# Three buffers instead of two for the weight-conversion tile, four instead of five for the activation's first temporary

## Chip, cores and metric

One core of one Trainium2 chip runs the whole program. The metric is the device time of one execution in microseconds, as a median over runs. The engines are TensorE (PE, with its weight loads as PEld), VectorE (DVE), ScalarE (ACT), GpSimd (POOL) and SyncE (SP), which issues every DMA here.

## What is computed

A causal attention with a multiplicative decay is followed by two dense feed-forward layers. The weights of the layers come as 64-bit floats, which the kernel itself turns into 32-bit floats.

```python
scores = q @ k.T / sqrt(D) + (cum[i] - cum[j])      # cum = cumsum(log f), causal
x = softmax(scores) @ v                             # 4 batches, 8 heads, 576 x 64
h = x @ w_in1                                       # 2304 x 512 @ 512 x 2048
x = where(h >= 1, h, where(h <= -1, 0, (h+1)**2/4)) @ w_out1
h = x @ w_in2
out = (P(h) / (Q(h) + 1e-6)) @ w_out2               # P cubic, Q quadratic in |h|
```

## The kernel before

Every product that must be exact to about 32 bits is made of three matmuls: each operand is split into a high part (a cast to fp32r on ACT) and a low part (a subtraction on DVE or POOL), and wl·xh, wh·xl and wh·xh are accumulated in PSUM.

**Attention** works on 16 pairs of heads, 9 blocks of rows each. **The first layer** is tiled into 16 groups g of 128 hidden columns and five chunks x of tokens (four of 512, one of 256). For one chunk and one group, `gemm_in` (L735) makes the hidden tile h in PSUM with 12 matmuls, an activation follows, `split_g_hi` (L745) and `split_g_lo` (L749) split the result, and `gemm_out` (L829, in the second layer L831) adds 12 matmuls to the output accumulators. Groups 0 to 3 of chunks 0 and 1 are done during the attention; their `gemm_out` is L816. After the attention come groups 0 to 3 of chunks 2 and 3, then groups 4 to 15 of chunks 0 to 3, then the short chunk, then the second layer, chunk after chunk. One chunk's input is split by L720 (ACT, xh) and L724 (DVE, xl), one step for each of four slices kk. The split tiles have one buffer each, so the next chunk's steps wait until the last group's `gemm_in` of the chunk before has read the slice.

**Weights.** A unit is one half (0: w_in, 1: w_out) of one group's weights. `w_raw` (L83) loads the 512 KB of its 64-bit words into a tile "raw", of which there are two. `w_steps` makes 32-bit floats of it: s0 (L93, ACT) takes a tile "d" and writes the absolute value's upper word, s1 to s4 (L97, L101, L107, L113, all DVE) work on it in place, and s4 frees raw. Then one of two things happens. Either the unit is split at once: L127 (ACT) writes wh and L131 (POOL) writes wl from it, and L131 frees d. Or the unit is stored to DRAM by L140, and d is free when the store has landed; `w_load` (L145) brings it back later, half 0 into a "d" tile and half 1 into a "raw" tile, and L127 and L131 split it. Units of groups 0 to 3 of layer 1 (8 units) are converted and split in the attention, groups 4 to 8 (10 units) are converted and stored there. After the attention groups 9 to 15 (14 units) are converted and split, and the 32 units of layer 2 are converted and stored; these are loaded again while the short chunk runs.

**Activation temporaries.** In the first layer `a11` (L754, DVE) takes a tile t0 for the clamped h, `a12` (L759, ACT) squares it into t1, which is the last use of t0, and `a21` (L763, DVE) is the last reader of h. In the second layer `b_abs` (L770, ACT) takes t0, t1 and t2; the last reader of t0 is `b_ln`/`b_exp` (L791, L794, ACT), and h is last read by `b_t4` (L805, DVE). h has four buffers (HB = 4) after the attention.

**Order.** Nothing is reordered by hand. Each piece of work is a task with an engine, an assumed duration, a key (its turn), tasks it depends on, and tags of buffers that it takes and frees. `plan` goes through simulated time and takes, again and again, the task with the smallest start time plus a small weight times its key; a task that takes a tag can't start before a buffer of it is free. The counts of buffers in `N_BUF` and in `bufs.update` are thus the planner's picture of the pools. The engines' programs are emitted in the planned order, once for the attention with what is mixed into it, and once for all that follows. On the chip every engine runs its program in order, and waits by semaphores where a tile is still in use.

```python
free_at = max(free_at, sorted(bufs[tag])[k - 1])
...
at = max(clock[eng], free_at)
...
cand = (choice[1] + turn + wk * key, key, n, choice[1], choice[2])
```

The keys of the units: a unit of the attention is loaded with its key less 6 and stored with its key plus 3; a unit of layer 2 has key base + 20 + i, is loaded with that less 4 and stored with that plus 1. Successive units of the attention that are stored are 6.4 apart in key.

Of the kernel before, what the change touches and what calls it, by code (L numbers as in the profile page):

```python
# [7 lines left out]
F32 = mybir.dt.float32  # L8
# [10 lines left out]
def kernel(ctx, tc, qT, kT, v, f, w_in1, w_out1, w_in2, w_out2, a, b, out):  # L19
    nc = tc.nc  # L20
    PE, ACT, DVE, POOL, SP = nc.tensor, nc.scalar, nc.vector, nc.gpsimd, nc.sync
    B, H, S = f.shape
    D = v.shape[2] // 2
    NT, DM = out.shape
# [4 lines left out]
    P = 128  # L29
# [11 lines left out]
    W_EARLY = 4  # L41
# [2 lines left out]
    CM, CE = 80, 144  # L44
    PB = 6
    FILL = 2
    SB, TB_, OB, RB = 4, 2, 2, 2
    KM, KEX, KT, KC, KV, KR, KX, PKL, LK, FE, FS = 0.0, 1.0, 4.0, 4.0, 7.0, 2.0, 9.0, 7.0, 14.0, 170.0, 40.0
    I_K, I_Q = 4.4, 5.2
# [27 lines left out]
    wpool = {}  # L77
# [8 lines left out]
    def w_steps(m, g, half):  # L86

        at = {}

        def s0():  # L90
            at["t"] = wst.pop((m, g, half))
            at["d"] = wpool["stage"].tile([P, DM], F32, tag="d", name="wd", bufs=2)
            ACT.activation(at["d"][:], at["t"][:, :, 1].bitcast(F32), AF.Abs)  # L93

        def s1():
            d = at["d"][:]
            DVE.tensor_scalar(out=d, in0=d, scalar1=W_MIN, scalar2=W_MAX, op0=ALU.max, op1=ALU.min)  # L97

        def s2():
            di = at["d"][:].bitcast(I32)  # L100
            DVE.tensor_scalar(  # L101
                out=di, in0=di, scalar1=3, scalar2=0x3FFFFFF8, op0=ALU.logical_shift_left, op1=ALU.bitwise_and
            )

        def s3():
            di = at["d"][:].bitcast(I32)
            DVE.scalar_tensor_tensor(  # L107
                out=di, in0=at["t"][:, :, 1], scalar=-1073741824, in1=di, op0=ALU.bitwise_and, op1=ALU.bitwise_or
            )

        def s4():
            di = at["d"][:].bitcast(I32)
            DVE.scalar_tensor_tensor(  # L113
                out=di, in0=at["t"][:, :, 0], scalar=29, in1=di, op0=ALU.logical_shift_right, op1=ALU.bitwise_or
            )
            wst[m, g, half] = at["d"][:]

        return [s0, s1, s2, s3, s4]

    def w_split(m, g, half):  # L120
# [20 lines left out]

    def w_load(m, g, half):
        tag, shape = (("d", [P, DM]), ("raw", [P, 2 * DM]))[half]
        t = wpool["stage"].tile(shape, F32, tag=tag, name=f"wf{m}_{g}_{half}", bufs=2)[:, 0:DM]
        SP.dma_start(t, wfd[m, g, half])  # L145
        wst[m, g, half] = t

# [2 lines left out]
    stage = wpool["stage"] = ctx.enter_context(tc.tile_pool(name="stage", bufs=1))  # L150
# [19 lines left out]
    for j in range(2):  # L170
        t = tri2[j * QB:(j + 1) * QB, 192:256]
# [13 lines left out]
    cb = [ap1.tile([P, 3, S], F32, name=f"cb{n}") for n in range(2)]  # L185
# [9 lines left out]
    half = ap1.tile([P, 2], F32, name="half")  # L195
# [51 lines left out]
    SF = 4  # L247
    XR = 4
    XA = 3
    KMK = 2.0  # L250
    LX = 4.0
    T0 = 1.5
    N_BUF = dict(S=SB, T=TB_, O=OB, P=PB, PT0=1, PT1=1, q=2, k=2, qs=2, ks=2, v=2, R=RB, x=1, cb=2, g=W_EARLY, c=2, s=SF, xa=XA, xr=XR, po=2, raw=2, d=2)
    LAT = {"pe": 0.2, "act": 0.2, "dve": 0.2, "pool": 0.2, "sp": 0.0, "init": 0.0}

    def task(key, eng, dur, fn, deps=(), take=(), free=()):
# [6 lines left out]
    shape = {}  # L263
# [7 lines left out]
    bufs = {}  # L271
# [94 lines left out]
    xa = {}  # L366
# [310 lines left out]
    t = task(-99, "init", 1.0, lambda: None)  # L677
    t = task(-99, "pe", 0.4 * WARM, lambda: warm(WARM), (t,), ("T",), ("T",))
    task(-99, "pe", 0.22 * WARM2, lambda: warm(WARM2), (t,), ("T",), ("T",))
    x = ft[:, 0, :].bitcast(F32)  # L680
    t = task(-99, "init", 2.86, lambda: None)
    t = task(-99, "dve", 0.37, lambda x=x: f_clip(x), (t,))
    t = task(-99, "act", 0.57, lambda x=x: ACT.activation(x, x, AF.Ln), (t,))
    t = task(-99, "dve", 1.35, lambda x=x: f_scan(cum, x), (t,))
    t = task(-99, "act", 0.57, c_hi, (t,))
    t2 = task(-98, "act", 0.57, c_all, (t,))
    t = tid[0, "c"] = task(-99, "dve", 0.67, c_lo, (t,))
# [3 lines left out]
    t = task(20, "sp", [(0.55, 0.01)] * 2, ab_load)  # L691
    t = task(24, "act", 0.4, ab_fn, (t,))
    for e, fn in root_steps():
        t = task(30, e, 0.3 if e == "act" else 0.17, fn, (t,))
# [31 lines left out]
    hps, gt, mid, acc, po = {}, {}, {}, {}, {}  # L726
# [24 lines left out]
    def a11(g, n):  # L751
        c = t_new(g, "t0", n, 2 if filling else TN[0])
        s = t_new(g, "t1", n, SF if filling else TN[1])
        DVE.tensor_scalar(out=c, in0=hps[g], scalar1=-1.0, scalar2=1.0, op0=ALU.max, op1=ALU.min)  # L754
        mid[g] = [s, c]
# [117 lines left out]
    wd, stored = {}, {}  # L873
# [15 lines left out]
    for n, u in enumerate(units):  # L889
# [3 lines left out]
        t = convert(u, key, step, 6)  # L893
# [8 lines left out]
    pieces = []  # L902
    for x in range(FILL):
        pieces += [(CH[x] / 4, "x", x, kk) for kk in range(KD)]
# [5 lines left out]
    for size, kind, x, k in pieces:  # L910
# [3 lines left out]
        if kind == "x":  # L914
            t = xload = task(key - LX, "sp", ld(n), lambda x=x, k=k: x_load(x, k), xstores(x, k) + [xload], ("xr",))
            t = task(key, "act", cost("act", n), lambda x=x, k=k: split_x_hi(x, k), [t] + ([fid[kind, x, 0]] if k else []), ("x",) if k == 0 else ())
            fid[kind, x, k] = task(key, "dve", cost("dve", n), lambda x=x, k=k: split_x_lo(x, k), (t,), (), ("xr",))
        elif kind == "g":
            deps = [fid["x", x, kk] for kk in range(KD)] + [wd[0, k, 0], fid.get((kind, x - 1, k)), fid.get(("in", x, k - 1))]
            t = None  # L920
            for kk in range(KD):
                t = task(key, "pe", mm(n, 3), lambda x=x, k=k, kk=kk: gemm_in(0, x, k, (kk,)), deps if t is None else (t,),
                         ("O",) if t is None else (), ("x",) if k == W_EARLY - 1 and kk == KD - 1 else ())
            fid["in", x, k] = t
            t = task(key, "dve", cost("dve", n), lambda k=k, n=n: a11(k, n), (t,), ("c", "s"))
            t = task(key, "act", cost("act", n), lambda k=k: a12(k), (t,), (), ("c",))
            t = task(key, "dve", cost("dve", n), lambda k=k: a21(k), (t,), (), ("O",))
            t = task(key, "act", cost("act", n), lambda k=k, n=n: split_g_hi(k, n), (t,), ("g",))
            fid[kind, x, k] = task(key, "pool", cost("pool", n), lambda k=k: split_g_lo(k, POOL), (t,), (), ("s",))
        else:  # L930
            deps = [fid["g", x, g] for g in early] + [wd[0, g, 1] for g in early] + [fid.get((kind, x, k - 1))]
            t = None
            for part in range(3):
                t = task(key, "pe", mm(n, W_EARLY), lambda x=x, k=k, part=part: gemm_out1(x, early, k, part),
                         deps if t is None else (t,), ("O",) if t is None else (), ("g",) * W_EARLY if k == KD - 1 and part == 2 else ())
            fid[kind, x, k] = t
            t = task(key, "act", cost("act", n, "ps"), lambda x=x, k=k: part_out(x, k), (t,), ("po",), ("O",))
# [3 lines left out]
    for kk in range(KD):  # L941
        n = CH[FILL]
        t = xload = task(FE + PX, "sp", ld(n), lambda kk=kk: x_load(FILL, kk), xstores(FILL, kk) + [xload], ("xr",))
        t = task(FE + PX, "act", cost("act", n), lambda kk=kk: split_x_hi(FILL, kk), [t] + sx0[:1], ("x",) if kk == 0 else ())
        sx0.append(task(FE + PX, "dve", cost("dve", n), lambda kk=kk: split_x_lo(FILL, kk), (t,), (), ("xr",)))
    TN = 5, 5, 5
    GB = 3
    HB = 4
    KO = 4, 8
# [11 lines left out]

    bufs.update({tag: [T0] * n for tag, n in N_BUF.items()})
    order_ = plan(0, WK)
# [10 lines left out]

    passes = [(0, x, early) for x in range(FILL, HEAD)] + [(0, x, late) for x in range(HEAD)]
    passes += [(0, x, range(NF)) for x in range(HEAD, NCH)]
# [12 lines left out]
    base = NS  # L989
    t_end = max(done[tid[NPAIR - 1, f"O{g}"]] for g in range(2)) + 0.2  # L990
    bufs.clear()
    bufs.update({tag: [t_end] * k for tag, k in dict(h=HB, g=GB, t0=TN[0], t1=TN[1], t2=TN[2], raw=2, d=2, xr=XR, a0=1, a1=1, a2=1, a3=1).items()})
    bufs.update({f"x{k}": [] for k in range(KD)})


# [1 line left out]
    for i, u in enumerate(units):  # L997
        g, half = u[1:]
        key = base + max(-1.0, min(needs[0, g] + 1.5 * half - CL, i * CK))
        if u in stored:  # L1000
            t = task(key, "sp", ld(DM), lambda u=u: w_load(*u), (stored[u],), (("d", "raw")[half],))
# [12 lines left out]
    for p, (m, x, fs) in enumerate(passes):  # L1014
# [6 lines left out]
        for kk in range(KD) if p else ():  # L1021
            deps = [evac[x - NCH, kk]] if m == 1 else xstores(x, kk)
            t = xload = task(k0 - KXL, "sp", ld(n), lambda x=x, kk=kk: x_load(x, kk), deps + [xload], ("xr",))
            t = task(k0 - 0.5, "act", ca, lambda x=x, kk=kk: split_x_hi(x, kk), [t] + sx[:1], (f"x{kk}",))
# [10 lines left out]
        for g in fs:  # L1035
# [7 lines left out]
            t = tin = prev_in  # L1043

            if m == 0:
                t = task(key, "dve", cd, lambda g=g, n=n: a11(g, n), (t,), ("t0", "t1"))
                t = task(key, "act", ca, lambda g=g: a12(g), (t,), (), ("t0",))
                t = task(key, "dve", cd, lambda g=g: a21(g), (t,), (), ("h",))
            else:
# [4 lines left out]
                t1 = task(key, "dve", cd, lambda g=g: b_t1(g), (tb,))  # L1054
                t1 = task(key, "dve", cd + 0.06, lambda g=g: b_t2(g), (t1,))
# [4 lines left out]
                t = task(key, "dve", cd, lambda g=g: b_t4(g), (t3, v3), (), ("h",))  # L1060
            t = task(key, "act", ca, lambda g=g, n=n: split_g_hi(g, n), (t,), ("g",))
            t = task(key, "pool", cp, lambda g=g: split_g_lo(g, POOL), (t,), (), ("t1",))
# [22 lines left out]
            if m == 0 and uses[0, g][0] == p:  # L1085

                for half in range(2):
                    k = base + min(sizes[p, g] + 1.5 * half + 0.5, needs[1, g] + KO[1] * half - W2L)
                    tag = ("d", "raw")[half]
                    u = (1, g, half)  # L1090
                    t = task(k, "sp", ld(DM), lambda u=u: w_load(*u), tuple(stored.values()), (tag,))
# [52 lines left out]
```

## Time and profile before

| what | value |
|---|---|
| time, three runs | 985.03, 982.06, 983.71 us; median 983.71 us |
| profiled execution, first to last instruction | 984.3 us (its own time is not listed apart; the span is 0.6 us above the median of the runs) |
| instructions | 15503 |
| PE, DVE, ACT, POOL busy | 98%, 74%, 64%, 46% of the span |
| mean granted TensorE clock | 0.995 |
| DMA | 125.15 MB, mean 127 GB/s |

A busy share of 98% on PE says that some matmul was under way nearly always. Matmuls overlap in the trace, so whether they follow one another at the usual distance is read from the distance of their starts, or from the chain of waits, where 12 of them take 2.72 us when nothing is late. In all views times are microseconds from the first instruction.

### The profile page before, as it was taken

Reading aid. Unit: us, or ns where it says so; the run is one execution under the profiler, and the core shown is the slowest. Engines: PE = TensorE matmul, PEld = TensorE weight load, DVE = VectorE, ACT = ScalarE, POOL = GpSimd, SP = SyncE. Lnnn points to the kernel's source line nnn. Section 1 sums busy time; section 2 is a strip of 40 time slices with the busy share of each in tenths; the row PEclk is TensorE's granted clock in tenths of the full one; section 3 lists DMA queues with packets and bytes.
Section 4 is the critical chain, followed back from the end, with each engine's and each line's share of the span. In section 5 each row is a group of like instructions: output and inputs, shape, how many; then the busy total and the mean of one; then the engine's idle time right before and its main releaser. Section 6 shows DMA issues by size and latency. Waiting matters only on the chain.

```text
span 984.3 us, 15503 instructions
## 1 busy us (share of the span) xinstructions
PE 964.6 (98%) x5124; PEld 784.3 (80%) x5124; DVE 729.0 (74%) x1379; ACT 629.6 (64%) x1324; POOL 457.0 (46%) x505
## 2 busy tenths in 40 slices
PE   8988999999999999999999999999999999999998
PEld 5656777777888788888888998888888888888887
DVE  7999888883876977877875679776667667666656
ACT  6988688884654433424333579776777667666666
POOL 4877746654655422222221225544444454444444
PEclk9999999999999999999999999999999999999999
DMA  6878589844563365665643651010101100010010
GB/s 224 260 258 251 174 272 293 263 162 166 194 232 118 96 226 155 188 205 161 221 151 123 177 172 33 1 44 1 43 1 44 43 1 22 0 43 1 1 44 22
DMA packets 66657, 125.15 MB, mean 127 GB/s; under 512 B 10048, under 2 KB 20944, under 8 KB 66576
## 3 DMA queue, kind: packets, MB, share of 16 engines
q1 hardware_dynamic: 66576, 124.16, 39.6%
q8 instruction: 40, 0.66, 0.3%
q14 instruction: 41, 0.34, 0.1%
HBM read 94.61 MB, written 29.51 MB: 126 GB/s over the span
## 4 chain that ended last, share of the span: by engine, by line
PE 85%; DVE 6%; DMA 3%; issue 2%; ACT 2%; SPq 1%; POOL 1%; DVEq 0%; POOLq 0%; ACTq 0%
PE h L735 38%; PE a L831 19%; PE a L829 17%; PE T L510 3%; PE O L547 2%; PE a L816 2%; PE S L446 2%; DVE P L486 1%; DVE xl L724 1%; DMA cb<-cd 1%; DMA R<-rcd 1%; PE S L437 1%; ACT P L498 1%; DVE wd L97 1%; DVE PT L360 0%
## 5 line engine op out<-in xcount | busy, mean ns | idle before, releaser
L749 POOL TENSOR_TENSOR gl<-t,gh 128x512 fp32r<-128x512 f32 (+1 forms) x160 | 195.4, 1222 | 292.1 <-ACT gh L745 224.8
L735 PE MATMUL h<-xl,wh 128*128 128x512 f32 (+1 forms) x640 | 236.7, 370 | 1.0 <-DVE xl L724 0.6
L735 PE MATMUL h<-xh,wl 128*128 128x512 f32 (+1 forms) x640 | 237.0, 370 | 0.0
L735 PE MATMUL h<-xh,wh 128*128 128x512 f32 (+1 forms) x640 | 235.7, 368 | 0.0
L745 ACT CAST gh<-t 128x512 fp32r<-128x512 f32 (+1 forms) x160 | 92.9, 581 | 124.0 <-PE a L831 47.9
L780 POOL TENSOR_TENSOR t<-t,t 128x512 f32<-128x512 f32 (+1 forms) x80 | 94.5, 1182 | 126.7 <-ACT t L773 121.1
L735 PEld LDWEIGHTS h<-xl,wh 128*128 128x128 f32 x640 | 120.8, 189 | 24.0 <-DVE xl L724 4.2
L735 PEld LDWEIGHTS h<-xh,wl 128*128 128x128 f32 x640 | 120.9, 189 | 20.4
L735 PEld LDWEIGHTS h<-xh,wh 128*128 128x128 f32 x640 | 120.8, 189 | 19.9
L831 PE MATMUL a<-wh,gl 128*128 128x512 f32 x288 | 112.3, 390 | 0.3 <-POOL gl L749 0.3
L831 PE MATMUL a<-wl,gh 128*128 128x512 f32 x288 | 112.2, 390 | 0.0
L831 PE MATMUL a<-wh,gh 128*128 128x512 f32 x288 | 112.1, 389 | 0.0
L829 PE MATMUL a<-gh,wl 128*128 128x512 f32 (+1 forms) x288 | 105.3, 366 | 0.0
L829 PE MATMUL a<-gl,wh 128*128 128x512 f32 (+1 forms) x288 | 105.3, 366 | 0.0
L829 PE MATMUL a<-gh,wh 128*128 128x512 f32 (+1 forms) x288 | 105.2, 365 | 0.0
L759 ACT ACTIVATE t<-t 128x512 f32<-128x512 f32 (+1 forms) x80 | 47.1, 589 | 83.5 <-DVE t L754 82.7
L798 DVE SCALAR_TENSOR_TENSOR t<-t,na,h 128x512 f32<-128x512 f32 (+1 forms) x80 | 55.4, 693 | 57.2 <-ACT h L794 56.1
L498 ACT ACTIVATE P<-P,nm 128x576 f32<-128x576 f32 (+2 forms) x144 | 83.6, 582 | 16.4 <-DVE nm L486 15.5
L754 DVE TENSOR_SCALAR t<-h 128x512 f32<-128x512 f32 (+1 forms) x80 | 50.6, 634 | 53.7 <-PE h L735 53.1
L784 DVE TENSOR_TENSOR t<-h,t 128x512 f32<-128x512 f32 (+1 forms) x80 | 51.0, 637 | 49.0 <-ACT t L776 48.6
L770 ACT ACTIVATE t<-h,ab 128x512 f32<-128x512 f32 (+1 forms) x80 | 51.8, 649 | 42.1 <-PE h L735 41.9
L238 POOL TENSOR_SCALAR_AFFINE_SELECT cb<-cb 128x128 f32<-128x128 f32 (+1 forms) x150 | 55.5, 381 | 43.7 <-DVE nm L486 33.9
(121 smaller groups left out, 1929.6 us busy)
## 6 DMA issues: line engine op xcount, KB each, us to landing
raw<-in_moe_w_in_dram SPq DMA_DIRECT2D x32, 512.0 KB
raw<-in_moe_w_out_dram SPq DMA_DIRECT2D x32, 512.0 KB
xr<-xd SPq DMA_DIRECT2D x48, 256.0 KB
wfd<-wd SPq DMA_DIRECT2D x42, 256.0 KB
wf<-wfd SPq DMA_DIRECT2D x42, 256.0 KB
cb<-cd SPq DMA_DIRECT2D x15, 576.0 KB
ks<-in_k_dram SPq DMA_DIRECT2D x16, 288.0 KB
qs<-in_q_dram SPq DMA_DIRECT2D x16, 288.0 KB
```

The costliest lines, as they stand in the source:

```text
L238: POOL.affine_select(out=t, in_=t, compare_op=ALU.is_ge, fill=-BIG, base=0, pattern=[[-1, n]], channel_multiplier=1,)
L498: ACT.activation(p, p, AF.Exp, scale=-1.0, bias=nm[pr][:, pos:pos + 1], accum_out=ls[pr][:, COL[pos]:COL[pos] + 1])
L735: PE.matmul(hps[g], ww[:, kk * P:(kk + 1) * P], xx[kk], start=(kk == 0 and y == 0), stop=(kk == KD - 1 and y == 2))
L745: ACT.copy(gt[g][0], mid[g][0])
L749: eng.tensor_tensor(out=lo, in0=mid.pop(g)[0], in1=hi.bitcast(F32), op=ALU.subtract)
L754: DVE.tensor_scalar(out=c, in0=hps[g], scalar1=-1.0, scalar2=1.0, op0=ALU.max, op1=ALU.min)
L770: ACT.activation(mid[g]["w"], hps[g], AF.Abs, scale=ab[:, 0:1])
L780: POOL.tensor_tensor(out=vv, in0=vv, in1=mid[g]["w"], op=ALU.add)
L784: DVE.tensor_tensor(out=t, in0=hps[g], in1=t, op=ALU.mult)
L798: DVE.scalar_tensor_tensor(out=t, in0=t, scalar=na[:, 0:1], in1=hps[g], op0=ALU.add, op1=ALU.mult)
L829: PE.matmul(acc[x, d], ww[:, dd], gg, start=st, stop=sp)
L831: PE.matmul(acc[x, d], gg[:, dd], ww[:], start=st, stop=sp)
```

## The change

The tile d gets a third buffer, in the pool and in the planner's picture of both parts. The tag t0 goes from five buffers to four in the part after the attention. One buffer of either is 2 KB of each partition. No instruction is added or removed.

```diff
+    DB = 3
...
-            at["d"] = wpool["stage"].tile([P, DM], F32, tag="d", name="wd", bufs=2)
+            at["d"] = wpool["stage"].tile([P, DM], F32, tag="d", name="wd", bufs=DB)
...
-        t = wpool["stage"].tile(shape, F32, tag=tag, name=f"wf{m}_{g}_{half}", bufs=2)[:, 0:DM]
+        t = wpool["stage"].tile(shape, F32, tag=tag, name=f"wf{m}_{g}_{half}", bufs=(DB, 2)[half])[:, 0:DM]
...
-    N_BUF = dict(S=SB, ..., po=2, raw=2, d=2)
+    N_BUF = dict(S=SB, ..., po=2, raw=2, d=DB)
...
-    TN = 5, 5, 5
+    TN = 4, 5, 5
...
-    bufs.update({tag: [t_end] * k for tag, k in dict(h=HB, g=GB, t0=TN[0], ..., raw=2, d=2, xr=XR, ...).items()})
+    bufs.update({tag: [t_end] * k for tag, k in dict(h=HB, g=GB, t0=TN[0], ..., raw=2, d=DB, xr=XR, ...).items()})
```

## Rows read from the trace of the kernel before

**Rows 1.** Busy time by stretch: window, length, engines' busy time (instructions), clock, DMA

```profile
0.00:225.00 225.00, 210.26 (x1526) 151.81 (x1528) 195.49 (x549) 185.46 (x529) 145.15 (x248) 0.98 0.75 237
225.00:984.30 759.30, 754.36 (x3600) 632.49 (x3596) 533.46 (x831) 444.11 (x796) 311.85 (x257) 1.00 0.30 95
```

**Rows 2.** The same view, five shorter windows

```profile
50.00:75.00 25.00, 21.69 (x164) 14.65 (x164) 24.65 (x68) 21.61 (x64) 18.87 (x31) 0.95 0.76 251
400.00:425.00 25.00, 25.00 (x112) 20.68 (x111) 21.02 (x34) 8.49 (x14) 6.72 (x5) 1.00 0.68 221
980.70:984.30 3.60, 0.00 (x0) 0.00 (x0) 0.69 (x1) 0.00 (x0) 0.00 (x0) 0.95 0.39 146
...
232.90:345.00 112.10, 111.45 (x488) 90.77 (x488) 84.80 (x117) 59.96 (x104) 61.64 (x45) 1.00 0.50 166
345.00:531.00 186.00, 186.00 (x822) 154.04 (x821) 139.15 (x216) 66.62 (x110) 46.17 (x35) 1.00 0.58 182
```

**Rows 3.** Waits of PE, 225 to 984 us: total, times, longest

```profile
PE h L735 <- DVE xl L724: 0.6, 1, 0.6
PE a L831 <- POOL gl L749: 0.3, 1, 0.3
```

**Rows 4.** The chain that ended last, 330 to 344 us and 403 to 407 us

```profile
330.74 2.73 PE h L735 x12
...
335.01 1.52 DVE wd L97
...
337.04 2.99 DVE xl L724 x3
...
340.08 3.48 PE h L735 x14
...
404.76 0.68 PE h L735 x3
```

**Rows 5.** Instructions of tile wd: durations min/median/max in ns, first and last start

```profile
L93 ACT ACTIVATE wd<-raw x64: 644/666/693, 21.7 to 513.5; 128x512 f32<-128x512 f32 x64
L97 DVE TENSOR_SCALAR wd<-wd x64: 410/421/1668, 23.3 to 514.9; 128x512 f32<-128x512 f32 x64
L101 DVE TENSOR_SCALAR wd<-wd x64: 409/426/1456, 24.2 to 515.4; 128x512 int32<-128x512 int32 x64
L107 DVE SCALAR_TENSOR_TENSOR wd<-raw,wd x64: 674/693/1959, 25.0 to 515.8; 128x512 int32<-128x512 int32 x64
L113 DVE SCALAR_TENSOR_TENSOR wd<-raw,wd x64: 642/686/1910, 26.5 to 518.3; 128x512 int32<-128x512 int32 x64
```

**Rows 6.** Waits of ACT on d, 232 to 345 us and 345 to 531 us

```profile
ACT wd L93 <- POOL wl L131: 2.1, 2, 1.2
...
ACT wd L93 <- DMA wfd<-wd: 7.0, 6, 1.9
```

**Rows 7.** Timelines of POOL, ACT and SP, attention: when d came free, when it was taken

```profile
29.17 1.28 POOL L131 TENSOR_TENSOR wl<-wd,wh 128x512 fp32r<-128x512 f32 x1
...
35.44 0.66 ACT L93 ACTIVATE wd<-raw 128x512 f32<-128x512 f32 x1
...
165.46 0.33 SPq L140 DMA_DIRECT2D wfd<-wd  x1
165.83 1.51 SPq L83 DMA_DIRECT2D raw<-in_moe_w_in_dram  x1
...
176.05 0.68 ACT L93 ACTIVATE wd<-raw 128x512 f32<-128x512 f32 x1
```

**Rows 8.** The SP timeline at 342 us

```profile
342.32 0.33 SPq L83 DMA_DIRECT2D raw<-in_moe_w_in_dram  x1
342.69 0.43 SPq L140 DMA_DIRECT2D wfd<-wd  x1
```

**Rows 9.** The DVE timeline, the last two xl of a chunk's start

```profile
402.28 1.30 DVE L97 TENSOR_SCALAR wd<-wd 128x512 f32<-128x512 f32 x1
403.50 0.68 DVE L724 TENSOR_TENSOR xl<-xr,xh 128x512 fp32r<-128x512 f32 x1
```

**Rows 10.** Waits of whole engines on h, total us, times, longest

```profile
DVE t L754 <- PE h L735: 53.1, 40, 9.7
ACT t L770 <- PE h L735: 41.9, 49, 1.8
```

More of the change, by code (lines that the diff above doesn't have):

```diff
@@ L252 @@
     T0 = 1.5
-    N_BUF = dict(S=SB, T=TB_, O=OB, P=PB, PT0=1, PT1=1, q=2, k=2, qs=2, ks=2, v=2, R=RB, x=1, cb=2, g=W_EARLY, c=2, s=SF, xa=XA, xr=XR, po=2, raw=2, d=2)
+    N_BUF = dict(S=SB, T=TB_, O=OB, P=PB, PT0=1, PT1=1, q=2, k=2, qs=2, ks=2, v=2, R=RB, x=1, cb=2, g=W_EARLY, c=2, s=SF, xa=XA, xr=XR, po=2, raw=2, d=DB)
     LAT = {"pe": 0.2, "act": 0.2, "dve": 0.2, "pool": 0.2, "sp": 0.0, "init": 0.0}
@@ L991 @@
     bufs.clear()
-    bufs.update({tag: [t_end] * k for tag, k in dict(h=HB, g=GB, t0=TN[0], t1=TN[1], t2=TN[2], raw=2, d=2, xr=XR, a0=1, a1=1, a2=1, a3=1).items()})
+    bufs.update({tag: [t_end] * k for tag, k in dict(h=HB, g=GB, t0=TN[0], t1=TN[1], t2=TN[2], raw=2, d=DB, xr=XR, a0=1, a1=1, a2=1, a3=1).items()})
     bufs.update({f"x{k}": [] for k in range(KD)})
```

## The prediction

> **What bounds the kernel now.** I read the windows first, then PE's waits, then the chain, and only then the tile that is changed. The windows split the execution in two [rows 1]. Up to 225 us, the attention, PE is busy 210.26 of 225.00 us, so 14.74 us are open; one stretch of it has DVE busy 24.65 of 25 us [rows 2], so VectorE is the tight engine there. From 225 us on PE is busy 754.36 of 759.30 us. Of the 4.94 us that are open, 3.60 lie behind the last matmul, at 980.7 us [rows 2], where the last output is copied and stored. That leaves 1.34 us of visible idle time in 755.7 us.
>
> Busy time alone could hide a slow pace, so the pace has to be looked at as well. In a stretch without a stall 112 matmuls of 512 columns start in 25 us [rows 2], and in the chain 12 of them take 2.73 us [rows 4], 0.227 us each, at a granted clock of 1.00 (2.4 GHz). PE waited twice in that whole part, 0.6 and 0.3 us [rows 3]. So after the attention the kernel is bound by TensorE at its own pace, and another engine matters only where it makes PE late. The one such place is the start of chunk 0's successor. The last `gemm_in` ends at 333.47 us (330.74 + 2.73) and the next one starts at 340.08 [rows 4]; in these 6.61 us PE had 25 matmuls of `gemm_out` left by the trace's count, 5.67 us at 0.227, and so lost 0.94 us by pace, of which 0.6 shows as a wait [rows 3]. On DVE a step of a weight conversion, L97, lies in the middle of the four xl that PE waits for, and takes 1.52 us [rows 4] against a median of 0.42 [rows 5].
>
> **The third d, in the attention.** It saves something only where an Abs step (L93) found no free d, on the chip or in the plan. On the chip none of the 18 Abs there waited on d: no such wait is in that stretch. The nearest one took d 4.99 us after it was free (35.44 less 29.17 + 1.28 [rows 7]). In the plan the reason is structural. Abs of unit n also needs raw of unit n, whose load can't be issued before s4 of unit n−2 has freed a raw buffer, and there are still two of those. For the stored units the store of n−2 has the smaller key (+3 against 12.8 − 6 = +6.8 for the load), so it goes out first, as at 165.46 and 165.83 us [rows 7], and is the smaller transfer; d is then free before raw has landed, and the third buffer is never asked for. For the eight units that are split at once, d is free after L127 and L131, normally before or about when a 512 KB load has landed, and Abs came later still. So I expect the same plan for the attention, the same instructions in the same order, and a cost of 0. The cover is those 4.99 us; if it is gone in the plan, the order of all that follows may change, which is a rival below.
>
> **The third d, after the attention.** Here it does bind. In 232 to 345 us Abs waited twice for a wl to free d, 2.1 us in all, and in 345 to 531 us six times for a store to land, 7.0 us in all [rows 6]. The order on SP is the reason for the second: for layer 2 the load's key is below the store's (n − 4 against n − 2 + 1), so the load goes out first and the store behind it, 342.32 and 342.69 us [rows 8]; d comes free last. With a third d these 9.1 us of waiting on ACT go, and the planner may also start the first raw conversions earlier, because the loads of stored units no longer hold both d. What is late next is raw, still two. The work is the same: 64 conversions of 0.67 us on ACT and 0.42 + 0.43 + 0.69 + 0.69 = 2.23 us on DVE by medians [rows 5], only sooner. ACT's 9.1 us are hidden under PE, which had no idle time at all in 345 to 531 us, and 0.65 us in 232.9 to 345 [rows 2]. They are worth nothing by themselves. What can be won is the 0.94 us at 333 us: the weights of the last groups would be ready sooner, so the planner need not spend `gemm_out` ahead of the last `gemm_in`, and the start of the next chunk is covered again. What can be lost is the same kind of thing at the other chunk starts. Bounds: a gain between 0 and 1.34 us, and a loss from 0 to one late start (priced below). As the stall may go and a smaller one may come elsewhere, I take half: a gain of 0.4 us.
>
> In the short chunk (531 to 605 us) half 0 of each unit is loaded into d, so three instead of two can be in flight. PE is not waiting there [rows 3]; 0 us, and a loss would have to come through the same xl steps.
>
> **Four t0 instead of five.** A t0 lives inside the life of its h: it is taken after `gemm_in` has filled h and is last read before the last reader of h. h has four buffers, so at most four t0 are live, and the fifth group's `gemm_in` already waits for the h of the first, which is freed after its t0. No wait can be added, in the plan or on the chip. The trace agrees as far as it can: what L770 and L754 wait for is h from PE, 41.9 and 53.1 us [rows 10]. The value is 0; a loss is excluded by the order of the steps, a gain by the fact that nothing is taken away.
>
> **The sum.** From the span 984.3: attention 0, ACT's waits 0, PE's chunk starts −0.4, t0 0, giving a span of 983.9. The median of the runs lies 0.6 below the span (983.71), so the forecast for the median is **983.3 us**. What the three runs differ by, 982.06 to 985.03, is 0.3%, and I take 0.3% of 983.7, 2.95 us, as what a measurement of this kernel can tell from no change.
>
> **Rivals.** *Slower: conversions in front of the xl steps.* With a third d the next conversion is allowed to run sooner on DVE, and engines run in order. At the chunk start of 400 us the last xl ends at 403.50 + 0.68 = 404.18 [rows 9] and PE takes that slice at 404.76 [rows 4]: 0.58 us of cover. One more conversion ahead of that xl is 2.23 us on DVE, or 3.48 if one of its steps is of the slow kind (1.67 − 0.42 = 1.25 us more [rows 5]). PE would lose 3.48 − 0.58 = 2.9 us, and the time would be 986.6; two such places give 989.5. It decides from one whole conversion at one start. For it: DVE is busy 84.80 of 112.10 us where the first 14 conversions run [rows 2], and the 1.30 us step at 402.28 already lies right before an xl [rows 9]. Against it: the planner sees xl and its own order of PE, raw still limits how far conversions run ahead, and 27.3 us of DVE are free there.
>
> The slow steps themselves have a rule. The Trainium skill, "SBUF — State Buffer", section "Who interferes with whom", says that VectorE and GpSimd share one pair of ports, held exclusively for a whole instruction, so that the loser blocks. By it a third d does harm, since a conversion on VectorE may then run beside the wl step of the one before on GpSimd, which two buffers kept apart. If every one of the 14 conversions lost 1.25 us [rows 5] this way, DVE would have 17.5 us more, below its 27.3 free, so by that rule too only the chunk starts decide, at the price above, and the sum by rows stays as it is.
>
> *Faster: the attention's plan changes after all.* If the plan let an Abs wait for d where the chip did not, its order changes from there on. Of 14.74 us idle on PE [rows 1] a fifth would be 2.95 us, 980.3 us. Against it are the structure above, the missing waits, and DVE at 24.65 of 25 us: an earlier conversion brings no relief to it and could as well cost.
>
> *No change at all.* The plan after the attention changes, but the chunk starts come out as before: 983.7. This lies within my forecast's bound and is counted with it.
>
> **Chances.** PE-bound, within 2.95 us either way: 0.77. Slower by the xl rival, including a worse order in the attention: 0.14. Faster by a changed attention: 0.09. The range takes in the full gain of 1.34 (982.4) and some scatter of the median below it, and above it one late start: **981.2 to 986.6**.
>
> **What the profile afterwards would show.** Right: the same attention, instruction for instruction; no Abs waiting on wl or on a store; the last conversion earlier than 513.5 us [rows 5]; PE busy about 754 of 759 us after 225 us; t0 never named in a wait. Wrong: more than 1 us of PE waiting on xl at a chunk start (slower rival), or another order of the L93 steps before 225 us and a different end of the attention (faster rival, or slower).

## The result, and the profile after

The changed kernel takes 989.9 us (median of 6 runs, 988.14 to 992.59) against 983.84 us for the kernel before beside it: a ratio of 1.0069, 95% interval 1.0051 to 1.0087. It is slower, where no change was forecast, and it lies outside the predicted range. The execution that is profiled has a span of 990.9 us; it is the slowest of the six, with the lowest mean granted clock, 0.991, and the three with a mean of 0.997 or 0.998 took 988.14 to 988.69 us. Its line numbers behind line 46 are one higher than before (L735 is now L736).

First the windows, as in [rows 1] and [rows 2]: window, length, busy time of PE, PEld, DVE, ACT, POOL (instructions), clock, DMA share, GB/s.

```profile
0.00:225.00 225.00, 212.26 (x1532) 152.57 (x1534) 194.65 (x550) 185.83 (x529) 145.52 (x248) 0.98 0.76 237
225.00:990.90 765.90, 758.15 (x3596) 633.99 (x3592) 541.66 (x830) 445.16 (x795) 312.77 (x257) 0.99 0.29 94
250.00:275.00 25.00, 22.22 (x81) 16.99 (x81) 19.51 (x26) 12.21 (x21) 11.06 (x9) 0.86 0.46 158
...
275.00:300.00 25.00, 24.77 (x107) 19.49 (x107) 20.29 (x24) 13.89 (x25) 15.11 (x11) 1.00 0.65 208
```

The attention did not get worse. One stretch did: 250 to 275 us, with 81 matmuls where an undisturbed stretch has 112 [rows 2] and the kernel before has 109 there. The waits of PE from 225 us on name the steps (total, times, longest), where [rows 3] had 0.6 us of xl and 0.3 of gl:

```profile
PE h L736 <- DVE xl L725: 2.0, 4, 0.6
PE h L736 <- ACT xh L721: 1.4, 1, 1.4
```

PE's own timeline, where the last slice of chunk 3 is taken (start, duration, engine, line, tiles, and what ended the idle time before):

```profile
257.32 0.40 PE L830 MATMUL a<-gh,wh 128*128 128x512 f32 x1
259.10 0.80 PE L736 MATMUL h<-xh,wl 128*128 128x512 f32 x1 [1.38 <-ACT xh L721]
260.24 0.80 PE L736 MATMUL h<-xl,wh 128*128 128x512 f32 x1 [0.34 <-DVE xl L725]
...
265.93 0.39 PE L736 MATMUL h<-xh,wh 128*128 128x512 f32 x1
```

Two losses lie here. The slice is late, and then 13 matmuls, from 260.24 to 265.93, take 5.69 us, where 13 at 0.227 us [rows 4] take 2.95. The granted clock was 0.50 in 260 to 264 us, the lower of the two levels (1.2 GHz; window, length, busy time of PE alone, clock, DMA share, GB/s):

```profile
260.00:264.00 4.00, 3.76 (x9) 0.50 0.79 237
264.00:268.00 4.00, 4.00 (x15) 0.76 0.84 314
```

**A ruler that leaves the attention out.** The end of the attention moves by up to 4.4 us between the profiled executions, although its instructions stand in the same order on every engine in all kernels told of here. So I count from T, the start of the attention's last O matmuls, to the last matmul. Timeline rows of PE, the kernel before, then the changed one:

```profile
224.16 2.93 PE L547 MATMUL O<-PT,vt 128*64 128x320 f32 x28
...
980.28 0.39 PE L831 MATMUL a<-wh,gh 128*128 128x512 f32 x1
```

```profile
223.52 2.93 PE L548 MATMUL O<-PT,vt 128*64 128x320 f32 x28
...
986.80 0.39 PE L832 MATMUL a<-wh,gh 128*128 128x512 f32 x1
```

From T it is 756.12 us before and 763.28 after: 7.16 us lost. PE takes the last slice of chunk 3 at 257.02 before, T + 32.86, and at 260.24 after, T + 36.72, with the same 158 matmuls started since T: 3.86 us. The slow pace adds 5.69 − 2.95 = 2.74. The other 0.56 is what is left, chunk 0's start among it (107 matmuls in 275 to 300 us).

The half clock belongs to the profiled execution and not to every one. A clock of 0.86 over 25.00 us (250 to 275 us above) is 0.14 × 25.00 = 3.5 us, 0.0035 of the span, while an execution with a mean of 0.997 or 0.998 has lost only 0.002 to 0.003 in all. By this estimate those three lack that stretch, in full or in part. They took 4.3 to 4.9 us more than 983.84, and 7.16 − 2.74 is 4.42.

**Why the slice is late.** VectorE's timeline in front of that slice, before:

```profile
247.78 0.69 DVE L724 TENSOR_TENSOR xl<-xr,xh 128x512 fp32r<-128x512 f32 x1 [1.72 <-ACT xh L720]
248.60 1.30 DVE L97 TENSOR_SCALAR wd<-wd 128x512 f32<-128x512 f32 x1
249.94 1.40 DVE L101 TENSOR_SCALAR wd<-wd 128x512 int32<-128x512 int32 x1
251.37 0.69 DVE L107 SCALAR_TENSOR_TENSOR wd<-raw,wd 128x512 int32<-128x512 int32 x1
252.10 0.69 DVE L113 SCALAR_TENSOR_TENSOR wd<-raw,wd 128x512 int32<-128x512 int32 x1
252.71 0.68 DVE L724 TENSOR_TENSOR xl<-xr,xh 128x512 fp32r<-128x512 f32 x1
```

and after:

```profile
248.86 1.78 DVE L725 TENSOR_TENSOR xl<-xr,xh 128x512 fp32r<-128x512 f32 x1
250.56 1.77 DVE L108 SCALAR_TENSOR_TENSOR wd<-raw,wd 128x512 int32<-128x512 int32 x1
...
253.89 1.74 DVE L108 SCALAR_TENSOR_TENSOR wd<-raw,wd 128x512 int32<-128x512 int32 x1
255.56 0.68 DVE L725 TENSOR_TENSOR xl<-xr,xh 128x512 fp32r<-128x512 f32 x1
...
259.50 0.69 DVE L725 TENSOR_TENSOR xl<-xr,xh 128x512 fp32r<-128x512 f32 x1
```

From the first to the fourth xl of the chunk there are 10 conversion steps after, 5 before. The 10 last 9.40 us in all; by the medians of [rows 5] they would be 5.3. ScalarE shows why they are there. Its Abs steps stand at T + 23.73, 30.69 and 33.21 before, and at T + 22.47, 24.38 and 33.88 after: the second no longer waits for a d, and the conversion steps that follow it come ahead of the slices. The order on ScalarE changed with them. The third slice's xh stood ahead of the first unit's cast wh and now stands behind it, and that cast waits 4.53 us for VectorE. The last slice's xh stood ahead of the copies of chunk 2's results (t<-a) and now stands behind them, behind the second unit's cast and behind the third Abs. ScalarE before, then after:

```profile
255.43 0.60 ACT L720 CAST xh<-xr 128x512 fp32r<-128x512 f32 x1
255.94 1.55 ACT L358 COPY t<-a 128x512 f32<-128x512 f32 x3
```

```profile
245.99 0.67 ACT L94 ACTIVATE wd<-raw 128x512 f32<-128x512 f32 x1 [0.41 <-POOL wl L132]
...
247.90 0.67 ACT L94 ACTIVATE wd<-raw 128x512 f32<-128x512 f32 x1 [0.22 <-DMA raw<-in_moe_w_in_dram]
253.09 0.62 ACT L128 CAST wh<-wd 128x512 fp32r<-128x512 f32 x1 [4.53 <-DVE wd L114]
253.62 0.62 ACT L721 CAST xh<-xr 128x512 fp32r<-128x512 f32 x1
254.20 1.95 ACT L359 COPY t<-a 128x512 f32<-128x512 f32 x3
...
258.43 0.62 ACT L721 CAST xh<-xr 128x512 fp32r<-128x512 f32 x1
```

### The profile page after: what moved, and what is told of

Same layout as the page of the kernel before. It is cut to its first block, busy times and chain, and to the rows that moved or that the text cites. A ratio compares the mean times of both kernels' runs of the same rounds, so it can differ in the third digit from the quotient of the medians.

```text
span 990.9 us, 15503 instructions
## 1 busy us (share of the span) xinstructions
PE 970.4 (98%) x5124; PEld 786.6 (79%) x5124; DVE 736.3 (74%) x1379; ACT 631.0 (64%) x1324; POOL 458.3 (46%) x505
## 4 chain that ended last, share of the span: by engine, by line
PE 80%; DVE 7%; issue 4%; DMA 4%; ACT 2%; POOL 2%; SPq 0%; POOLq 0%; DVEq 0%; ACTq 0%
PE h L736 37%; PE a L832 19%; PE a L830 16%; PE T L511 3%; PE a L817 2%; PE O L548 2%; DVE xl L725 2%; PE S L447 1%; DVE P L487 1%; DVE wd L98 1%; DMA R<-rcd 1%; DMA ks<-in_k_dram 1%; DMA raw<-in_moe_w_out_dram 1%; POOL cb L239 1%; PE S L438 1%
## 5 line engine op out<-in xcount | busy, mean ns | idle before, releaser
L736 PE MATMUL h<-xl,wh 128*128 128x512 f32 (+1 forms) x640 | 238.0, 372 | 2.7 <-DVE xl L725 2.0
L736 PE MATMUL h<-xh,wl 128*128 128x512 f32 (+1 forms) x640 | 238.0, 372 | 1.4 <-ACT xh L721 1.4
L736 PE MATMUL h<-xh,wh 128*128 128x512 f32 (+1 forms) x640 | 236.6, 370 | 0.0
L736 PEld LDWEIGHTS h<-xl,wh 128*128 128x128 f32 x640 | 121.4, 190 | 27.4 <-DVE xl L725 7.4
L736 PEld LDWEIGHTS h<-xh,wl 128*128 128x128 f32 x640 | 121.3, 189 | 22.6 <-ACT xh L721 1.8
L736 PEld LDWEIGHTS h<-xh,wh 128*128 128x128 f32 x640 | 121.3, 190 | 19.6
```

Of the source, the lines that this page charges most:

```text
L736: PE.matmul(hps[g], ww[:, kk * P:(kk + 1) * P], xx[kk], start=(kk == 0 and y == 0), stop=(kk == KD - 1 and y == 2))
```

## The experiments

T to end is from each profiled execution as above, ratios are to the kernel before on the same chip.

| run | median us | ratio (95%) | T to end, us |
|---|---|---|---|
| before | 983.84 | 1 | 756.12 |
| the change | 989.9 | 1.0069 (1.0051 to 1.0087) | 763.28 |
| e1_four_t0 | 983.97 | 0.9995 (0.9981 to 1.0009) | 756.07 |
| e3_third_d_old_order | 983.6 | 0.9990 (0.9976 to 1.0004) | 755.75 |
| e5_x_ahead | 992.1 | 1.0078 (1.0058 to 1.0098) | 766.15 |
| e7_splits_ahead | 994.68 | 1.0105 (1.0086 to 1.0125) | 767.11 |
| e12_behind_chunk3 | 1000.42 | 1.0160 (1.0138 to 1.0182) | 773.96 |
| e13_behind_chunks3_0 | 999.31 | 1.0151 (1.0132 to 1.0171) | 770.68 |
| e10_wl_constant | 984.77 | 1.0014 (0.9999 to 1.0029) | 756.94 |
| e15_x_sooner | 983.43 | 0.9993 (0.9980 to 1.0005) | 755.68 |
| e6_x_loads_ahead | 991.13 | 1.0074 (1.0057 to 1.0091) | 765.02 |
| e18_six_wl_constant | 986.28 | 1.0027 (1.0015 to 1.0039) | 759.27 |
| e17_before_wl_constant | 981.9 | 0.9981 (0.9969 to 0.9993) | 754.88 |
| e16_before_x_sooner | 979.3 | 0.9958 (0.9945 to 0.9971) | 752.73 |
| e19_three_memsets | 986.73 | 1.0043 (1.0027 to 1.0060) | 758.65 |
| e20_wh_minus_wh | 985.33 | 1.0022 (1.0009 to 1.0035) | 758.98 |

**Each part by itself.** Four t0 with two d:

```diff
-    DB = 3
+    DB = 2
```

> The edit of the first temporary alone: four t0, but two buffers for d as before. Every engine's program comes out in the order of the kernel before. Theory A (the third d makes the planner put conversion steps ahead of the steps that split the next chunk's input, and PE starves at that chunk's start): same as before, 983.8 within 3. Theory C (a fifth t0 was needed): slower, towards the 989.9 of the changed kernel.

No change. Then the third d in the pool and four t0, but the planner of the second part told of two d, so that the order is the one of before:

```diff
-    bufs.update({..., raw=2, d=DB, ...
+    bufs.update({..., raw=2, d=2, ...
```

> Three buffers for d on the chip and four t0, but the planner is told of two d for the part after the attention, so that every engine's program has the order of the kernel before. Theory A (the order alone): 983.8 within 3, the chunk start at 244 to 257 us without a stall. Theory B (the third buffer itself: other addresses, conversions that run beside GpSimd's steps): slower than before by most of the 6.1, 987 to 990.

No change either. From 345 to 531 us Abs waits 7.3 us on stores in the run with two d, and here on none of them; it is worth nothing. The loss needs the new order.

**The x steps moved ahead by hand.** The planned order of the changed kernel is kept, and only chunk 3's loads, xh and xl (first run), or its xh and xl (second), are put as early as their inputs allow.

```diff
+        for kk in range(KD):                    # chunk p = 1, the one after chunk 2
+            load, hi, lo = xt[p, kk]
+            put(hi, [load, free[kk]] + [m for k in range(kk) for m in xt[p, k][1:2]])
+            put(lo, [hi] + [m for k in range(kk) for m in xt[p, k][2:]])
```

> The changed kernel, in which the loads and both split steps of chunk 3's input (xr, xh, xl; 12 instructions) are emitted ahead of the conversions, in all three queues; PE's and POOL's programs are untouched. Theory A: the 3.3 us that the last xl came late and the 2.3 us at half clock behind it go; 5 us or more of the 6.1, so 983 to 985.5. What stays is the smaller stall at the next chunk's start (about 1 us). Theory B: no change, 989.9 within 1.5.

> As the run with loads and splits ahead, but only the split steps xh and xl move on ScalarE and VectorE; the loads keep their places behind the conversion's raw loads on the DMA queue. If the two in-order engines make the delay: PE gets its last slice 2 to 3 us sooner, 984 to 986.5. If the DMA queue makes it (the last xr load is issued at 253.5 us, behind a raw load that waits for a conversion to end): the last xl comes no sooner than about 258.5 us, so 1 to 2 us are won, 987.5 to 989.

Both missed: neither is faster than the change itself. PE's waits in the first of them:

```profile
PE h L736 <- DVE xl L725: 3.5, 2, 2.9
PE a L830 <- POOL gl L750: 3.1, 1, 3.1
```

The early x steps stand in front of the activation of chunk 2's last groups, so gl is late at 248.64 us, and the 2.9 us are the start of chunk 0, which the same conversions now make late. Moving one step in queues that are full moves the wait.

**The conversions moved behind.** The opposite: the conversion steps between a chunk's first load and its last xl go behind that xl, for chunk 3, and for chunks 3 and 0.

```diff
+        mid = order[i:j + 1]
+        return order[:i] + [t for t in mid if t[0] not in conv] + [t for t in mid if t[0] in conv] + order[j + 1:]
...
+    for p in (1,):                              # (1, 2) in the second run
+        order_ = behind(order_, p)
```

> The changed kernel with one thing moved: every step of a weight conversion that the planner's order puts between the first load and the last xl of chunk 3 now comes behind that last xl. The activation's steps stay where they are. Conversions-ahead theory (each PE stall at a chunk start is the conversions in front of the xl steps): the 3.3 us late start near 257 us and the half clock behind it (about 2.3 us) go, but chunk 0, the next, still has conversions ahead of its xl, now more of them, and pays there. 986 to 990, and PE waits on xl at one start, not two. Rival, scattered slow steps on VectorE set the delay, whatever the order: 989 to 991, with the stall near 257 us still there.

> As the run before it, for two chunk starts: the conversion steps among the loads and splits of chunk 3 and of chunk 0 go behind the last xl of each. Conversions-ahead theory: no PE wait on xl at either start, 983.5 to 985.5, unless the conversions now come too late for the group that needs them, which would show as a PE wait on wh or wl. Rival, slow VectorE steps: 987 to 990.

Missed by 10 us and more. The longest wait of PE in the first, from 225 us on:

```profile
PE a L830 <- POOL gl L750: 12.4, 1, 12.4
```

GpSimd keeps its order, with wl ahead of gl. A conversion that is put off puts off its wl, and every gl behind it. So the place of the conversions is bounded from both sides, and the times of these four runs decide nothing beyond that. Two of them show one thing more. With no conversion step between the first and the last xl of chunk 3, PE still took its last slice at T + 34.47 and T + 34.53, 1.6 and 1.7 us later than before, and waited 1.2 us for its xh, which stands behind the copies of chunk 2's results in these runs too. That part of the late start is ScalarE's order and not VectorE's conversions.

**GpSimd's subtraction out.** Same order, but GpSimd does not read:

```diff
+            if m == 0 and g >= W_EARLY:
+                eng.memset(lo[:].bitcast(F32), 0.0)
+            else:
                 eng.tensor_tensor(out=lo[:], in0=at["s"], in1=hi[:].bitcast(F32), op=ALU.subtract)
```

> The changed kernel, same order, with GpSimd's subtraction for the low part of layer 1's weights (groups 4 to 15) replaced by a memset of zero: the low part of those weights is left out. GpSimd then reads nothing for it and is busy for less. Port theory (VectorE's steps of 1.3 to 1.8 us are steps that had to wait for GpSimd's subtraction, and they make xl late): the slow steps of 244 to 260 us fall to 0.4 to 0.7 us each, the stall near 257 us shrinks by 2 us or more, 984 to 987. Order theory (the number of steps ahead of xl decides): 988 to 991.

The loss is all but gone, with the same 10 steps in front of the fourth xl. They take 5.32 us there, the medians, against 9.40; one of them, the third xl, and on ScalarE the copies that the last xh stands behind (lines shifted by the edit):

```profile
248.56 0.69 DVE L108 SCALAR_TENSOR_TENSOR wd<-raw,wd 128x512 int32<-128x512 int32 x1
249.17 0.68 DVE L728 TENSOR_TENSOR xl<-xr,xh 128x512 fp32r<-128x512 f32 x1
...
251.01 1.95 ACT L362 COPY t<-a 128x512 f32<-128x512 f32 x3 [2.10 <-PE a L833]
```

With T = 221.14 the third xl starts at T + 28.03, against 32.04 in the changed kernel and 28.55 before. The last slice does not come back in full: PE takes it at T + 34.67, against 36.72 and 32.86, after a wait of 1.4 us for its xh. Of the 3.86 us, then, 1.81 stay with the order alone and 2.05 go with the subtractions. The clock stayed at 1.00 here, so the 2.74 us went too. The order without the subtractions costs little from T, and the subtractions in the old order cost little too (the last run below); together they cost more than their sum.

**Only six of the subtractions out**, those that start between 242.9 and 257.6 us:

```diff
-            if m == 0 and g >= W_EARLY:
+            if m == 0 and (g, half) in ((4, 1), (6, 0), (7, 0), (8, 0), (9, 0), (10, 0)):
```

> The changed kernel, same order, with only six of GpSimd's wl subtractions replaced by a memset of zero, those that start between 242.9 and 257.6 us (the low part of these six weight tiles is left out). If the slow VectorE steps in these 17 us make chunk 3 late, the stall near 257 us goes as it did with all of them replaced, and only chunk 0's (about 1 us) is left: 985 to 987.5. If the gain of that run came from somewhere else, 988.5 to 991.

As expected: 763.28 − 759.27 = 4.0 of 7.16 us come back from six steps, the 2.74 of the half clock among them, since the clock stayed at 1.00. PE takes the last slice at T + 34.68, as with all of them out. The place is right.

**GpSimd as busy, reading nothing; and GpSimd reading, letting go sooner.** A memset is also shorter and waits for no wh. So it was made three times over, and in the other run the subtraction was kept with wh in the place of wd or wf.

```diff
+                for _ in range(3):
+                    eng.memset(lo[:].bitcast(F32), 0.0)
```

```diff
+                eng.tensor_tensor(out=lo[:], in0=hi[:].bitcast(F32), in1=hi[:].bitcast(F32), op=ALU.subtract)
```

> As the run with the constant low part, but the memset is made three times, 3 x 0.53 = 1.59 us, so GpSimd is busy for at least as long as with the subtraction (1.33 to 1.48 us) and still reads nothing (the low part of layer 1's weights, groups 4 to 15, is left out). If VectorE's two-input steps are held up by what GpSimd reads, they stay near 0.69 us and the time stays at 984 to 986. If it was GpSimd's time, 988 to 991.

> The changed kernel with GpSimd's subtraction for the same weights made as wh minus wh in place of wd (or wf) minus wh: the same kind of step, the same wait for wh, two tiles read, but wd is let go after ScalarE's cast (the low part is left out again, it is zero). If the gain came from GpSimd reading nothing, the slow steps and the stall near 257 us are back, 987.5 to 991. If it came from d being free sooner, 984 to 986.

The costs of VectorE's steps answer for the steps, grouped by line from 232 to 300 us (busy us, mean ns, idle before). The changed kernel:

```profile
L132 POOL TENSOR_TENSOR wl<-wf,wh 128x512 fp32r<-128x512 f32 x9 | 12.9, 1446 | 1.5 <-ACT wh L128 1.5
...
L108 DVE SCALAR_TENSOR_TENSOR wd<-raw,wd 128x512 int32<-128x512 int32 x7 | 8.0, 1136 | 0.0
...
L98 DVE TENSOR_SCALAR wd<-wd 128x512 f32<-128x512 f32 x7 | 6.1, 877 | 2.5 <-ACT wd L94 2.5
```

Three memsets:

```profile
L134 POOL MEMSET wl<- 128x512 f32 x51 | 27.9, 557 | 2.0
...
L98 DVE TENSOR_SCALAR wd<-wd 128x512 f32<-128x512 f32 x8 | 8.5, 1067 | 4.1 <-ACT wd L94 3.9
...
L114 DVE SCALAR_TENSOR_TENSOR wd<-raw,wd 128x512 int32<-128x512 int32 x8 | 6.6, 823 | 0.1
L108 DVE SCALAR_TENSOR_TENSOR wd<-raw,wd 128x512 int32<-128x512 int32 x8 | 5.4, 681 | 0.1
```

wh minus wh:

```profile
L133 POOL TENSOR_TENSOR wl<-wh 128x512 fp32r<-128x512 f32 x17 | 18.8, 1113 | 17.7 <-ACT wh L128 17.7
...
L108 DVE SCALAR_TENSOR_TENSOR wd<-raw,wd 128x512 int32<-128x512 int32 x8 | 7.0, 880 | 0.1
```

Beside memsets, with GpSimd busy for longer, the step with two inputs L108 is at its 0.68 us, while the step with one (L98) is slower than in the changed kernel. L114, which has two inputs as well, has a mean of 0.82, for GpSimd still makes the gl of the activation by a subtraction. Taken one by one, from T to T + 130 us, the steps separate. In the run with memsets all 16 two-input steps (L108, L114, xl) that overlapped memsets alone took 0.67 to 0.69 us, and the 15 that overlapped a subtraction 0.68 to 1.82. Of the 13 one-input steps (L98, L102) that overlapped memsets alone, 12 took 0.5 us or more, up to 0.82. With wh minus wh, a subtraction of one tile from itself, two-input steps took up to 1.82 us again. So it is GpSimd's reading that holds up the steps with two inputs, not its time. The Trainium skill, "SBUF — State Buffer", section "Who interferes with whom", says just this: a VectorE instruction with two SBUF inputs contends with a GpSimd instruction that reads SBUF and not with one that only writes, and one in a two-port mode contends with GpSimd. These steps agree, if L98 and L102 run in such a mode, which no row shows.

The times do not separate the theories. Three memsets came out at 986.73 us, 0.7 above the range of the reading theory and below that of the other, and the profiled execution is the fastest of its eight. It shows where GpSimd's time does cost: the memsets put off a gl, and PE waits for it and then, as in the other runs of this order, for the last xh.

```profile
PE h L740 <- ACT xh L725: 1.4, 1, 1.4
PE a L834 <- POOL gl L754: 1.3, 1, 1.3
```

PE takes the last slice at T + 36.40 there, nearly as late as in the changed kernel. Wh minus wh came out 2.2 us below the range that I had given to the reading theory, and inside the one for its rival, d being free sooner. Its subtraction takes 1.04 us a time where the full one takes 1.29 to 1.74, the third xl stands at T + 30.64, about halfway, and PE takes the last slice at T + 35.60. How much of its gain is the shorter subtraction and how much the earlier d is not shown. Neither profiled execution has the stretch at half clock; that alone is 2.74 us of the difference.

**Only the loads ahead.** Is it SP's queue that makes the slices late? The last slice's load stood there behind a raw load until 253.52 us (timeline of SP, changed kernel).

```profile
253.13 0.33 SPq L84 DMA_DIRECT2D raw<-in_moe_w_out_dram  x1
253.52 0.43 SPq L715 DMA_DIRECT2D xr<-xd  x1
```

```diff
+        for kk in range(KD):
+            n = xt[p, kk][0]
+            if at.index(n) > at.index(raws[0]):
+                at.remove(n)
+                at.insert(at.index(raws[0]), n)
```

> The changed kernel with chunk 3's four loads alone put ahead of the first raw load on SP's queue; the orders of VectorE and ScalarE stay. If SP's queue made the slices late (the load of the last slice 3.5 us later than before, behind a raw load that waited for L114), the start near 257 us is covered again: 985 to 987. If the conversions ahead of xl on VectorE set it, as the two runs above suggest, the loads lie ready and nothing is won: 988.5 to 991.

Nothing is won; it came out 0.1 us above the range for that. The four loads were issued by 234.3 us, the 10 steps still took 9.31 us, and from the first xl to the fourth it is 14.85 us where the changed kernel has 15.56. SP's queue is not it. (The loads put ahead delay a load of weights, for which a cast wh waits 2.0 us, and the first xl comes 2.3 us later from T.)

**The planner told to prefer the x steps.** In place of moves by hand, a lower key, with the change and without it:

```diff
-            t = xload = task(k0 - KXL, "sp", ...
-            t = task(k0 - 0.5, "act", ...
-            sx.append(task(k0 - 0.5, "dve", ...
+            t = xload = task(k0 - KXL - 30, "sp", ...
+            t = task(k0 - 30.5, "act", ...
+            sx.append(task(k0 - 30.5, "dve", ...
```

> Both parts of the change kept, and the planner itself told to prefer the x steps: the keys of the next chunk's loads, xh and xl are lowered by 30, so that they go ahead of conversions whenever both could start. Conversions-ahead theory: PE waits on xl nowhere for more than 0.7 us, 983 to 985, the third buffer then worth nothing for the time. Rival, three buffers harm by themselves (more conversions in flight beside the attention's successor): 988 to 991.

> The kernel before (two d, five t0) with the keys of the x steps lowered by 30, as was done for three d. If the key alone repairs the chunk starts, it gives the same time with two d, 982.5 to 984.5, and the third buffer is worth nothing; if a third d is worth something once its harm is gone, this run is slower than that one by 0.5 to 2 us, 984 to 985.5.

With three d this repairs the change, to the time of before and no further. Its waits of PE, the one on xl just above the 0.7 us expected:

```profile
PE a L830 <- ACT t L359: 1.4, 1, 1.4
PE h L736 <- DVE xl L725: 0.8, 1, 0.8
```

With two d it beats both kernels, the one before by 0.42%. I had expected 982.5 us or more. PE waits nowhere behind 225 us there, and the window that held 109 matmuls before is full. The kernel before, then this run (PE alone):

```profile
250.00:275.00 25.00, 25.00 (x109) 19.95 (x108) 22.34 (x30) 14.83 (x27) 14.27 (x10) 1.00 0.55 189
```

```profile
250.00:275.00 25.00, 25.00 (x112) 1.00 0.64 203
```

From T it is 2.95 us shorter than with three d (755.68 − 752.73). Even with the x steps preferred the second Abs comes at T + 26.19 with three d and at T + 31.29 with two. The third buffer costs time here too, 0.9993 against 0.9958 of the kernel before.

**The slow steps in the kernel before.** The memset of e10 in the order of before:

```diff
+            if m == 0 and g >= W_EARLY:
+                eng.memset(lo[:].bitcast(F32), 0.0)
```

> The kernel before, with GpSimd's subtraction for the low part of layer 1's weights (groups 4 to 15) replaced by a memset of zero (that part of the weights is left out). If slow VectorE steps cost time only where a chunk start hangs on them, nothing can be won beyond the 0.94 us at 333 us: 982.5 to 984.5. If GpSimd's subtractions cost time everywhere, 979 to 981.

The median is 0.6 us below the first range and above the second: 1.24 us are won from T (756.12 − 754.88), in the changed kernel 6.34 (763.28 − 756.94), 2.74 of it the half clock of that execution. By the ratios it is 0.19% against 0.55%. The other way round, the new order costs 756.94 − 754.88 = 2.06 us from T without the subtractions (0.33% by the ratios) and 7.16 with them. Each costs something alone, and the larger part comes only with both. (In e10, e17, e18, e19 and e20 the low part of the weights named is left out.)

## Why the prediction was wrong

**What held.** The attention is the same, instruction for instruction. Four t0 cost nothing. Abs no longer waits for a store behind 345 us, and waits for raw instead, 11.2 + 5.8 = 17.0 us, all hidden; one wait for a wl is left, 0.4 us at 246 us. The last Abs starts at 511.4 instead of 513.5 us [rows 5]. The third buffer as such is harmless (e3).

**The step that failed** is the one for the third d after the attention, where the value taken was a gain of 0.4 us out of "a gain between 0 and 1.34 us, and a loss from 0 to one late start". It reasoned that with d free sooner the conversions come sooner and the starts of the chunks are better covered. The planner did run them sooner, but it put them in front of the slices of chunk 3, and of chunk 0, and on ScalarE it put the copies of chunk 2's results in front of the last xh. In place of the gain of 0.4 us, PE got that slice 3.86 us later, and 7.16 us were lost from T. The rival "conversions in front of the xl steps" described this, with a chance of 0.14, and named what would show it; its place was sought at the starts of 333 and 400 us, and not at 244 to 260 us, where the second Abs had waited for a d until T + 30.69. A buffer that makes a step wait also keeps it out of the queue of others. "The planner sees xl and its own order of PE", the argument against the rival, failed. The durations that the planner assumes for the 10 steps (0.65, 0.53, 0.86 and 0.9 us for L98, L102, L108 and L114) add up to 7.06 us, which is more than the 5.3 of the medians, and the steps took 9.40. With the subtractions out 2.05 of the 3.86 us go; why the planned order loses the other 1.81 even where the steps run at their medians, no run tests.

**The price was too low as well.** It gave 3.48 − 0.58 = 2.9 us for one conversion at one start. The slice came 3.86 us later, larger by a third, and behind the pause PE ran 13 matmuls at half the clock in the profiled execution, 2.74 us more. By the estimate above it is missing in executions of 988.14 to 988.69 us, and these lie above the range too. No row of before showed a pause of PE above 0.6 us in that part, and so none showed what follows one.

**The rule cited** was right in kind, and the use made of it was too narrow. The prediction said that "by that rule too only the chunk starts decide, at the price above". They did decide, but the slow steps set how late a start is: 2.06 us from T for the new order without GpSimd's subtractions, 7.16 with them. Nor did two buffers keep the conversions and wl apart, as was said there: steps of 1.30 and 1.40 us stand in front of that slice in the kernel before too, and 1.24 us are won there without the subtractions.

**The gain to be had was also read too small.** The 1.34 us of visible idle time are not all that could be won: e16 is 756.12 − 752.73 = 3.4 us faster from T. The rest is pace, as in the 109 matmuls in 250 to 275 us before against 112.

What is left open: why the clock fell behind some pauses and not behind others, next section, and how the loss of the run with three memsets, 0.43%, splits between GpSimd's time and the rest. With order and slow steps together, the part of the loss that neither makes alone can be given to neither.

## What to carry to other kernels

A buffer count that a planner reads is also a priority: one more buffer lets background work start sooner, and in queues that run in order that means in front of something else. Before adding one, look at which step waited for it, and at what stands behind that step in each queue at the places where the bounding engine has the least cover. Price a late start by the pause and by what the clock does behind it, and give the planner the durations that the steps have next to their neighbours.

## What was not expected of the hardware

The pause of PE in the changed kernel, 1.38 and 0.34 us next to each other behind a first 0.54, was followed by a granted clock of 0.50 in 260 to 264 us, and the level came back by 268 us. With the loads moved (e6) the same is seen, 0.77, 0.50 and 0.87 in the windows from 256 to 268 us, and behind the one wait of 3.1 us in e5, which ended at 248.64 us, it was 0.50 in 248 to 252 us and 0.70 in 252 to 256. In e10, e18, e19 and e20 PE stood idle for 1.6 to 3.0 us between 225 and 275 us, in the changed kernel for 2.8, and the clock of those four stayed at 1.00 throughout. The runs do not show what decides.

VectorE's steps of 0.42 to 0.69 us take up to 1.96 us, and GpSimd's subtraction 1.26 to 1.74 us. From T to T + 130 us no conversion step or xl that overlapped nothing on GpSimd took more than 0.70 us (before, the change, e10, e17, e18, e19 and e20).
